# Token affine per head pair, weight sums and attention steps moved: a block-sorted attention followed by a token and channel MLP

## The chip, the cores and the metric

The kernel runs on one core of one Trainium2 chip. Its engines work side by side, each with its own queue that is worked off in order: TensorE (PE: matrix products into PSUM; its weight loads are shown as PEld), VectorE (DVE), ScalarE (ACT), GpSimd (POOL), and SyncE (SP), which here does nothing but issue DMA transfers. The metric is the device time of one execution in microseconds (us), the median over several runs. A profile of one execution gives, instruction by instruction, when each engine worked and what it waited for.

## The reference

Two blocks, one after the other, over batch 4, 8 heads, 768 tokens, 64 channels a head (512 channels in all):

```python
# block-sorted attention: 8 blocks of 96 tokens in each head
P = sort_net                                  # [4, 8, 8, 8]
for _ in range(5):
    P = exp(P - max(P)); P = P / sum(P, -1); P = P / sum(P, -2)
k_sorted = einsum('bhij,bhjcd->bhicd', P, k_blocks)
v_sorted = einsum('bhij,bhjcd->bhicd', P, v_blocks)
x = softmax(q_block @ k_sorted_block.T / 8) @ v_sorted_block      # within a block

# token and channel MLP on x[4, 768, 512]
a1  = alpha1 * x + beta1
tok = einsum('ts,bsd->btd', w_tok, a1)        # over the 768 tokens
u   = x + lam * tok
a2  = alpha2 * u + beta2
ch  = relu(a2 @ w_ch1) @ w_ch2                # 512 -> 2048 -> 512
out = u + lam * ch
```

## The kernel before

**Tiling of the tokens.** [...] The attention works on blocks of 96 tokens: its result `x_of[b]` is a tile [128, 8, 512] whose rows 0 to 95 hold block k in plane k. The token product sums over 768 = 6 x 128 tokens, so planes 0 to 5 have to be full: rows 96 to 127 of plane k are filled with a third (32 rows) of block 6 or 7. `tails(x, lo, hi, eng)` (line 513) does that in three copies, the a-th from rows 32a to 32a+31 of planes 6 and 7 to rows 96 to 127 of planes a and a+3. The token weights are permuted to the same order at the start. `a1_of[b]` is a tile of the same form and holds alpha1 * x + beta1, already multiplied by lam and a constant gain of 64.

**Attention steps.** A batch has four head pairs g = 0 to 3, and each has two halves hf (blocks 0 to 3, 4 to 7). `score(b, g, hf)` (line 419) issues 8 matrix products and one exponential on ACT (tile `et`); `pv(b, g, hf)` (line 479) issues 8 products with the values `Vs`, then on DVE a reciprocal and a multiplication that writes x. Both take their PSUM from a pool `psA` of two buffers. After its x, `pv` puts the affine of its 96x4x128 corner (`first_affine`, line 443: a multiplication and an addition on DVE) into a list `late`. In batch 1 each `pv` empties the list (`flush`); in batches 2 and 3 `flush_one` (line 510) takes one entry at a given place.

**The channel part.** Its hidden layer is computed in two halves hf of 384 tokens: `h_unit` (line 761) is one of 16 hidden units (4 products, then a relu on ACT), with PSUM from a pool `psB` of four buffers, shared with the token products and the output products. The outputs of batch 0 are plain products (`ch_unit`, line 764: three row tiles kk in four parts each). Batches 1 to 3 use a scheme with seven products in place of eight for a pair of row tiles (`ch_pair`, line 829): it needs differences of the second weight matrix, made once on DVE (`block_weights`, line 796: eight differences of 128x1024 into the tiles TWa and TWb), and sums and differences of hidden tiles (`block_sums`, line 812: four DVE operations for each range lo to hi of 8, three pairs n = 0, 1, 2 a batch). In `ch_pair` the accumulator px is used for three products and pz for two; each later product waits until the addition on DVE (`add_out`, line 791) has read the one before. Half 0 has the pair n = 0, half 1 the pairs n = 1 and 2.

**The token layer.** `moe_tok(b, kt)` (line 713): six products over a1, then on DVE u = x + tok / 64, then on ACT a cast of u to f16. `moe_cross(b, hf)` (line 723) issues three DMA transposes of u on SP; `moe_affine(b, hf)` (line 730) makes the input a2T of the hidden units from them, four operations on DVE, or on ACT for half 1 of batches 1 to 3.

**Keys and values of the next batches.** `mix_v` (line 545) and `mix_k` (line 560), three of each a batch, multiply the raw values and keys with the sorting matrices; ACT copies the results out of PSUM (one cast for values, four for keys). `bounce_v` sends the mixed values to memory in two DMAs and `back_v` brings them back as `Vs`; `q_cross` transposes the queries in six DMAs; all of these are issued by SP. `loads` waits on POOL until `Vs` has come back and then loads the raw tensors of the batch after that.

**The order is written out by hand.** Every engine gets its instructions in program order. The main loop goes over b and hf; each (b, hf) runs its 16 hidden units and after unit i what is registered for (b, hf, "h", i); then the output products, and after each product (or part) what is registered for (b, hf, "c", n). `put(b, hf, kind, n, ...)` (line 963) registers. So attention of batch b is spread over the channel part of batch p = b - 1, key and value mixing of b over the output products of (p - 1, 1), and the token layer of b over (p, 1) and (b, 0). The places in question stand in lines 998 to 1041: `put(p, *at_, flush_one)` at 1016, the pairs of scores and values at 1009, the tails at 1017, `block_weights` at 1033, `block_sums` of pair 2 at 1040.

Of the kernel before, what the change touches and what calls it, by code (L numbers as in the profile page):

```python
# [16 lines left out]
def kernel(  # L17
# [24 lines left out]
    BLK = S // NB  # L42
# [400 lines left out]
    def first_affine(b, rows, kts, c):  # L443
        n = kts.stop - kts.start
        w = c.stop - c.start
        dst = a1_of[b][rows, kts, c]
        al, be = (
            t_[rows, c].unsqueeze(1).to_broadcast([rows.stop - rows.start, n, w]) for t_ in (alphaB, betaB)
        )
        dve.tensor_tensor(dst, x_of[b][rows, kts, c], al, ALU.mult)  # L450
        dve.tensor_tensor(dst, dst, be, ALU.add)
# [27 lines left out]
    def pv(b, g, hf):  # L479
        if g == 0 and hf == 0:  # L480
            x_of[b] = moep.tile([128, 8, C], F16, name="x128", tag="x128", bufs=1)
            a1_of[b] = moep.tile([128, 8, C], F16, name="a1", tag="a1", bufs=1)
        ps = psa([128, 2, 512], FT, "x_ps")[:].rearrange("p a (k d) -> p a k d", d=128)
        et = ets[(b, g, hf)][:].rearrange("p a i t -> p (a i t)")
        for ii in range(4):
            for h2 in range(2):
                lo = (4 * h2 + ii) * BLK
                w = min(128, 8 * BLK - lo)
                pe.matmul(
                    ps[0:w, h2, ii, 0:D + 1], et[0:BLK, lo:lo + w],  # L490
                    Vs[0:BLK, (2 * g + h2) * NB + 4 * hf + ii, 0:D + 1], start=True, stop=True,
                )
        rc = att.tile([128, 2, 4], FT, name="rcb", tag="rc", bufs=3)
        dve.reciprocal(rc[0:BLK], ps[0:BLK, :, :, D])
        dve.tensor_tensor(
            x_of[b][0:BLK, 4 * hf:4 * hf + 4, g * 128:(g + 1) * 128].rearrange("p k (a d) -> p k a d", a=2),
            ps[0:BLK, :, :, 0:D].rearrange("p a k d -> p k a d"),
            rc[0:BLK].rearrange("p a k -> p k a").unsqueeze(3).to_broadcast([BLK, 4, 2, D]), ALU.mult,
        )
        if b == 1:  # L500
            flush()
        late.append(lambda: first_affine(b, slice(0, BLK), slice(4 * hf, 4 * hf + 4), slice(g * 128, (g + 1) * 128)))

    late = []

    def flush():
        while late:
            late.pop(0)()
# [1 line left out]
    def flush_one():  # L510
        late.pop(0)()

    def tails(x, lo, hi, eng):
        flush()
        for a in range(3):
            eng(x[96:128, a:a + 4:3, lo:hi], x[32 * a:32 * a + 32, 6:8, lo:hi])

    def q_cross(b, kt):
        if kt == 0:
# [40 lines left out]
    def mix_k(b, n, engs):  # L560
        if n == 0:
            kT_of[b] = att.tile([128, H4, NB, BLK], F16, name="kT", tag="kT", bufs=1)
        ps = psa([128, 8, 128], FT, "kmix_ps")
        raw = raw_of[(b, 0)]
        for tp in range(8):
            pe.matmul(
                ps[:, tp, :], raw[:, 16 * n + 2 * tp:16 * n + 2 * tp + 2, :].rearrange("p t d -> p (t d)"),
                bigP[b][:].rearrange("p a t g i -> p (a t g i)"), start=True, stop=True,
            )
        dst = kT_of[b][:].rearrange("p g i (th tp par) -> p th (g i) tp par", th=2, par=2)  # L570
        for par in range(2):
            for h2 in range(2):
                engs[2 * par + h2](
                    dst[h2 * 64:h2 * 64 + 64, :, :, 8 * n:8 * n + 8, par],
                    ps[par * 64:par * 64 + 64, :, h2 * 64:h2 * 64 + 64].rearrange(
                        "p n (th c) -> p th c n", th=2
                    ),
                )
# [134 lines left out]
    def moe_tok(b, kt, ps):  # L713
        u32 = u_of[b]
        tok_part(b, kt, 0, C, ps)
        if b not in u16_of:
            u16_of[b] = moep.tile([128, NT, C], F16, name="u16", tag="u16", bufs=1)
        dve.scalar_tensor_tensor(
            u32[kt], tok_of[(b, kt)][:], 1.0 / GAIN, x_of[b][:, kt, :], op0=ALU.mult, op1=ALU.add,
        )  # L720
        act.copy(u16_of[b][:, kt, :], u32[kt])
# [8 lines left out]
    def moe_affine(b, hf):  # L730
        for ci in range(CT):
            affine(b, hf, ci, uT_of[(b, hf)][:, ci, :], act if b and hf else dve)
# [230 lines left out]
    def put(b, hf, kind, n, *todo):  # L963
        at.setdefault((b, hf, kind, n), []).extend(todo)
# [19 lines left out]
    for b in range(1, B):  # L984
        p = b - 1
        if b == 1:
            for n in range(3):
                put(0, 0, "h", 11 + n, lambda n=n: mix_v(1, n, act.copy))
                put(0, 0, "c", 3 + 3 * n, lambda n=n: mix_k(1, n, (act.copy,) * 4))
            put(0, 0, "h", 13, lambda: bounce_v(1))  # L990
            put(0, 0, "c", 1, lambda: back_v(1))
            for g in range(H4):
                put(0, 0, "c", (4, 7, 10, 10)[g], lambda g=g: q_turn_late(1, g, (dve.tensor_copy, act.copy)[g % 2]))
            put(0, 0, "c", 11, lambda: loads(2))
            seq = [("s", 0), ("s", 1), ("s", 2), ("p", 0), ("s", 3), ("p", 1), ("p", 2), ("s", 4), ("p", 3), ("s", 5),
                   ("p", 4), ("s", 6), ("p", 5), ("s", 7), ("p", 6), ("p", 7)]
            for at_, (kind, n) in enumerate(seq):
                put(0, 1, "h", at_, (lambda n=n: score(1, n // 2, n % 2, psa)) if kind == "s" else (lambda n=n: pv(1, n // 2, n % 2)))
        else:
            for n in range(3):  # L1000
                put(p - 1, 1, "c", 1 + n, lambda b=b, n=n: mix_v(b, n, act.copy))
                put(p - 1, 1, "c", 5 + (2, 3)[b - 2] * n, lambda b=b, n=n: mix_k(b, n, (act.copy,) * 4))
            put(p - 1, 1, "c", 3, lambda b=b: bounce_v(b))
            put(p - 1, 1, "c", 7, lambda b=b: back_v(b))
            for kt in range(NT):
                put(*((0, 1, "h", 13) if b == 2 else (1, 0, "c", 1)), lambda b=b, kt=kt: q_cross(b, kt))
            if b + 1 < B:
                put(p, 0, "h", 3, lambda b=b: loads(b + 1))
            for (kind, n), at_ in zip(
                pairs, ((0, "h", 1), (0, "h", 4), (0, "h", 6), (0, "h", 8), (0, "h", 10), (0, "h", 12), (0, "h", 14), (0, "c", 3)),  # L1010
            ):
                for i in range(2):
                    f = (lambda b=b, n=n + i: score(b, n // 2, n % 2, psa)) if kind == "s" else (lambda b=b, n=n + i: pv(b, n // 2, n % 2))
                    put(p, *at_, f)
            for at_ in ((0, "h", 7), (0, "h", 9), (0, "h", 11), (0, "h", 13), (0, "c", 1), (0, "c", 5), (1, "h", 0), (1, "h", 1)):
                put(p, *at_, flush_one)
        put(
            p, 1, "h", 15 if b == 1 else 2, lambda b=b: tails(a1_of[b], 0, C, dve.tensor_copy),
            lambda b=b: tails(x_of[b], 0, C, dve.tensor_copy),
        )  # L1020
        put(p, 1, "h", 3, lambda b=b: moe_start(b))
        for kt in range(3):
            put(p, 1, *(("c", 4) if b == 1 else ("h", 5 + 2 * kt)), lambda b=b, kt=kt: moe_tok(b, kt, psb))
        put(p, 1, *(("c", 4) if b == 1 else ("h", 9)), lambda b=b: moe_cross(b, 0))
        put(p, 1, "c", 8 if b == 1 else 6, lambda b=b: moe_affine(b, 0))
        for kt in range(3):
            put(b, 0, "h", 2 * kt, lambda b=b, kt=kt: moe_tok(b, 3 + kt, psb))
        put(b, 0, "h", 4, lambda b=b: moe_cross(b, 1))
        put(b, 0, "c", 0, lambda b=b: moe_affine(b, 1))

    for g, m in enumerate((12, 12, 13, 13)):
        put(0, 0, "h", m, lambda g=g: scale_weights(g))
    for n, at_ in enumerate(((0, 1, "h", 13), (0, 1, "h", 14), (0, 1, "h", 15), (0, 1, "c", 1), (0, 1, "c", 6), (0, 1, "c", 9), (0, 1, "c", 11), (1, 0, "h", 5))):
        put(*at_, lambda n=n: block_weights(n))
    for b in range(1, B):
        for hf in range(2):
            for at_, lo, hi in ((8, 0, 4), (14, 4, 7), (15, 7, 8)):
                at.setdefault((b, hf, "h", at_), []).insert(0, lambda b=b, hf=hf, lo=lo, hi=hi: block_sums(b, hf, lo, hi))
        put(b, 1, "h", 11, lambda b=b: block_sums(b, 2, 0, 4))
        for at_, lo in ((1, 4), (4, 6)):  # L1040
            put(b, 1, "c", at_, lambda b=b, lo=lo: block_sums(b, 2, lo, lo + 2))

    for m in range(3):
        h_part(0, 0, m, [0])
# [58 lines left out]
```

## Time and profile before

| | us |
|---|---|
| median of 3 runs (264.88 to 266.41) | 266.05 |
| the profiled execution | 265.02 |
| its span, first instruction to last | 263.2 |

| engine | busy, us | share of the span |
|---|---|---|
| TensorE (PE) | 248.8 | 95% |
| VectorE (DVE) | 180.0 | 68% |
| ScalarE (ACT) | 154.7 | 59% |
| GpSimd (POOL) | 44.1 | 17% |

The granted clock of TensorE was 1.0 throughout. How to read the lines that follow: all engines' instructions are recorded by one helper, so every line number is L65 (SPq is SyncE's queue, and its rows are DMA issues); an instruction is told by its tiles, "output <- inputs", with partitions x elements and type. On a timeline the first column is the start in us after the span's start, the second the length, and a bracket at the end is idle time ahead of it with what ended it. Neighbouring DVE instructions overlap by some 0.07 us at their ends, so that a price is better taken from start to start.

In time the kernel runs so: batch 0's attention and everything that is loaded once until about 35 us; the channel part of batch 0 until 103 (half 1 from 70, with batch 1's attention in it); batch 1 from 104 to 161 (half 0 with batch 2's attention to 132, half 1 after it); batch 2 from 161 to 216; batch 3 to the end.

### The profile page before, as it was taken

The numbers are of one execution on the slowest core, as the hardware profiler recorded it, in microseconds if no ns is written. First come the engines' busy times: TensorE is split into PE (matmuls) and PEld (weight loads), VectorE is DVE, ScalarE is ACT, GpSimd is POOL, SyncE is SP. The second block draws the span as 40 slices with busy tenths as digits, with TensorE's granted clock in tenths as the row PEclk, the third lists the DMA queues.
The fourth block names the chain that finished last, engine by engine and source line by source line (L and its number), as shares of the span: only waits on it lengthen the run. The fifth ranks groups of instructions, "written<-read, shape, count | busy, mean of one in ns | idle before, by whom it ended". The sixth has DMA issues, their size and how long they took to land.

```text
span 263.2 us, 5966 instructions
## 1 busy us (share of the span) xinstructions
PE 248.8 (95%) x2371; PEld 159.9 (61%) x2371; DVE 180.0 (68%) x473; ACT 154.7 (59%) x282; POOL 44.1 (17%) x67
## 2 busy tenths in 40 slices
PE   7998899999999998998999999998999999999994
PEld 3466565545556444555855797556756875686783
DVE  6796979486359973469996774289977862361863
ACT  3577766657987549777446578788156004747400
POOL 8759304400181000083000000000000000000000
PEclk9999999999999999999999999999999999999999
DMA  6999999998999956989972169500122123111022
GB/s 103 214 203 190 206 205 214 200 135 184 193 167 170 130 137 153 152 139 176 159 124 69 22 157 161 125 20 2 41 59 42 42 82 80 23 38 42 2 80 80
DMA packets 67535, 31.07 MB, mean 118 GB/s; under 512 B 56674, under 2 KB 63218, under 8 KB 67508
## 3 DMA queue, kind: packets, MB, share of 16 engines
q0 software_dynamic: 26352, 15.34, 44.8%
q1 hardware_dynamic: 41060, 15.33, 33.0%
q8 instruction: 18, 0.29, 0.4%
q14 instruction: 9, 0.07, 0.1%
q10 hardware_dynamic: 96, 0.03, 0.1%
HBM read 32.79 MB, written 8.65 MB: 157 GB/s over the span
## 4 chain that ended last, share of the span: by engine, by line
PE 53%; DVE 17%; ACT 4%; issue 2%; DMA 1%; SPq 0%; DVEq 0%; ACTq 0%
PE h_ps L65 21%; PE tok_ps L65 8%; PE px L65 6%; PE pz L65 5%; PE py L65 5%; DVE x L65 4%; DVE sums L65 4%; PE ch_ps L65 3%; DVE a L65 3%; DVE ost L65 2%; ACT et L65 2%; PE sc_ps L65 1%; DVE hTa L65 1%; ACT kT L65 1%; PE kmix_ps L65 1%
## 5 line engine op out<-in xcount | busy, mean ns | idle before, releaser
L65 PE MATMUL h_ps<-a2T,W1p 128*128 128x384 bf16 x512 | 94.5, 327 | 0.9 <-DVE a2T L65 0.9
L65 PEld LDWEIGHTS <-W1p 128*128 128x128 bf16 x512 | 47.7, 98 | 32.9 <-issue 1.8
L65 ACT ACTIVATE hTa<-h_ps 128x384 f16<-128x384 f32 x64 | 31.2, 493 | 32.3 <-PE h_ps L65 31.7
L65 ACT ACTIVATE hTb<-h_ps 128x384 f16<-128x384 f32 x64 | 31.1, 489 | 8.1 <-PE h_ps L65 8.1
L65 PE MATMUL tok_ps<-a,w_tokT 128*128 128x512 f16 x126 | 30.7, 379 | 0.6 <-DVE ost L65 0.6
L65 DVE SCALAR_TENSOR_TENSOR u<-tok_ps,x 128x512 f32<-128x512 f32 x21 | 14.4, 691 | 22.5 <-PE tok_ps L65 22.5
L65 ACT CAST kT<-kmix_ps 64x512 f16<-64x512 f32 x36 | 25.7, 713 | 6.3 <-PE kmix_ps L65 5.8
L65 ACT CAST u<-u 128x512 f16<-128x512 f32 x21 | 12.9, 617 | 24.5 <-DVE u L65 24.5
L65 ACT ACTIVATE et<-sc_ps 96x768 f16<-96x768 f32 (+1 forms) x32 | 25.0, 807 | 2.0 <-PE sc_ps L65 1.8
L65 PEld LDWEIGHTS <-sums 128*128 128x128 f16 x216 | 21.1, 98 | 5.7 <-issue 2.7
L65 PEld LDWEIGHTS <-hTb 128*128 128x128 f16 x200 | 18.7, 98 | 6.6 <-issue 0.8
L65 PEld LDWEIGHTS <-hTa 128*128 128x128 f16 x192 | 18.5, 98 | 6.6
L65 PEld LDWEIGHTS <-w_tokT 128*128 128x128 f16 x126 | 12.3, 98 | 14.1 <-issue 1.5
L65 DVE TENSOR_TENSOR sums<-hTa,hTb 128x512 f16<-128x512 f16 (+3 forms) x27 | 8.9, 329 | 12.1 <-ACT hTb L65 11.8
L65 DVE TENSOR_TENSOR x<-x_ps,rcb 96x512 f16<-96x512 f32 x24 | 16.5, 686 | 0.8
L65 POOL DMA_DIRECT2D qn<-in_q_dram x18 | 16.0, 906 | 5.3 <-DMA raw<-in_v_dram 4.8
L65 PEld LDWEIGHTS <-et 96*128 96x128 f16 (+4 forms) x288 | 12.1, 100 | 6.2 <-issue 2.3
L65 PE MATMUL x_ps<-Vs,et 96*128 96x65 f16 (+4 forms) x288 | 13.4, 195 | 2.5 <-ACT et L65 1.1
L65 DVE TENSOR_TENSOR a<-a,betaB 96x512 f16<-96x512 f16 (+1 forms) x28 | 12.3, 441 | 1.0
L65 DVE SCALAR_TENSOR_TENSOR ost<-px,u 128x256 f32<-128x256 f32 x27 | 11.2, 417 | 2.2 <-PE px L65 2.2
L65 PE MATMUL warm_ps<-wz 128*128 128x512 f16 x36 | 11.1, 441 | 1.2 <-DVE wz L65 1.2
L65 PE MATMUL ch_ps<-W2p,hTb 128*128 128x512 f16 x48 | 12.0, 379 | 0.2
(140 smaller groups left out, 354.3 us busy)
## 6 DMA issues: line engine op xcount, KB each, us to landing
out_dram<-ost SPq DMA_DIRECT2D x23, 192.0 KB, 2.5
raw<-in_v_dram POOLq DMA_DIRECT2D x6, 384.0 KB, 7.2
raw<-in_k_dram POOLq DMA_DIRECT2D x6, 384.0 KB, 9.8
qn<-in_q_dram POOLq DMA_DIRECT2D x18, 128.0 KB, 10.7
vscr<-mixed SPq DMA_DIRECT2D x6, 384.0 KB
Vs<-vscr SPq DMA_DIRECT2D x3, 768.0 KB
W1p<-in_moe_w_ch_dram POOLq DMA_DIRECT2D x4, 512.0 KB, 11.8
W2p<-in_moe_w_ch_dram POOLq DMA_DIRECT2D x4, 512.0 KB, 17.3
```

The lines of the kernel that those rows point to most:

```text
L65: ins = getattr(self.eng, name)(*args, **kwargs)
```

## The change

The affine is no longer made per half pair but once per head pair: the second `pv` of a pair registers three copies of x that fill the tails of that pair's 128 channels, and then one affine over all 128 rows and six planes. The six copies over all channels (three of a1, three of x) go. In batches 2 and 3 the entries are taken at other places. The scores and values of batches 2 and 3 stand at other units and steps, two of the steps now in the output products, and the last values in half 1. The eight weight differences go behind batch 1's token products, in two groups of four. The key mixes of batches 2 and 3 stand one or more steps earlier, the first three token products of batches 2 and 3 and their transposes two units later, the affine of half 1 two steps later, and the sums of pair 2 are cut otherwise.

```diff
@@ pv
         if b == 1:
             flush()
-        late.append(lambda: first_affine(b, slice(0, BLK), slice(4 * hf, 4 * hf + 4), slice(g * 128, (g + 1) * 128)))
+        if hf == 1:
+            c = slice(g * 128, (g + 1) * 128)
+            late.append(lambda: tails(x_of[b], c))
+            late.append(lambda: first_affine(b, slice(0, 128), slice(0, NT), c))
@@ tails
-    def tails(x, lo, hi, eng):
-        flush()
+    def tails(x, c):
         for a in range(3):
-            eng(x[96:128, a:a + 4:3, lo:hi], x[32 * a:32 * a + 32, 6:8, lo:hi])
+            dve.tensor_copy(x[96:128, a:a + 4:3, c], x[32 * a:32 * a + 32, 6:8, c])
@@ the places
-                put(p - 1, 1, "c", 5 + (2, 3)[b - 2] * n, lambda b=b, n=n: mix_k(b, n, (act.copy,) * 4))
+                put(p - 1, 1, "c", ((3, 6, 8), (4, 7, 10))[b - 2][n], lambda b=b, n=n: mix_k(b, n, (act.copy,) * 4))
...
-                pairs, ((0, "h", 1), (0, "h", 4), (0, "h", 6), (0, "h", 8), (0, "h", 10), (0, "h", 12), (0, "h", 14), (0, "c", 3)),
+                pairs, ((0, "h", 0), (0, "h", 3), (0, "h", 5), (0, "h", 8), (0, "h", 11), (0, "c", 0), (0, "c", 2), (1, "h", 1)),
...
-            for at_ in ((0, "h", 7), (0, "h", 9), (0, "h", 11), (0, "h", 13), (0, "c", 1), (0, "c", 5), (1, "h", 0), (1, "h", 1)):
+            for at_ in ((0, "h", 6), (0, "h", 7), (0, "h", 12), (0, "h", 13), (0, "c", 4), (0, "c", 5), (1, "h", 2), (1, "h", 3)):
                 put(p, *at_, flush_one)
-        put(
-            p, 1, "h", 15 if b == 1 else 2, lambda b=b: tails(a1_of[b], 0, C, dve.tensor_copy),
-            lambda b=b: tails(x_of[b], 0, C, dve.tensor_copy),
-        )
+        if b == 1:
+            put(p, 1, "h", 15, flush)
         put(p, 1, "h", 3, lambda b=b: moe_start(b))
         for kt in range(3):
-            put(p, 1, *(("c", 4) if b == 1 else ("h", 5 + 2 * kt)), lambda b=b, kt=kt: moe_tok(b, kt, psb))
-        put(p, 1, *(("c", 4) if b == 1 else ("h", 9)), lambda b=b: moe_cross(b, 0))
+            put(p, 1, *(("c", 4) if b == 1 else ("h", 7 + 2 * kt)), lambda b=b, kt=kt: moe_tok(b, kt, psb))
+        put(p, 1, *(("c", 4) if b == 1 else ("h", 11)), lambda b=b: moe_cross(b, 0))
...
-        put(b, 0, "c", 0, lambda b=b: moe_affine(b, 1))
+        put(b, 0, "c", 2, lambda b=b: moe_affine(b, 1))
...
-    for n, at_ in enumerate(((0, 1, "h", 13), (0, 1, "h", 14), (0, 1, "h", 15), (0, 1, "c", 1), (0, 1, "c", 6), (0, 1, "c", 9), (0, 1, "c", 11), (1, 0, "h", 5))):
+    for n, at_ in enumerate(((0, 1, "c", 7),) * 4 + ((0, 1, "c", 9),) * 4):
         put(*at_, lambda n=n: block_weights(n))
...
-        for at_, lo in ((1, 4), (4, 6)):
-            put(b, 1, "c", at_, lambda b=b, lo=lo: block_sums(b, 2, lo, lo + 2))
+        for at_, lo, hi in ((0, 4, 7), (5, 7, 8)):
+            put(b, 1, "c", at_, lambda b=b, lo=lo, hi=hi: block_sums(b, 2, lo, hi))
```

In the list of pairs, s0, s2, s4, s6 are the scores of head pairs 0 to 3 (both halves), p0, p2, p4, p6 their values, in the order s0, s2, p0, s4, p2, s6, p4, p6.

## The prediction

> **What bounds the kernel now.** I read the page's head first, then TensorE's (PE's) waits from 69 us on, where the diff begins to act, and then the timelines of VectorE (DVE) and SyncE's queue (SPq) at each wait.
>
> ```profile
> span 263.2 us, 5966 instructions
> PE 248.8 (95%) x2371; PEld 159.9 (61%) x2371; DVE 180.0 (68%) x473; ACT 154.7 (59%) x282; POOL 44.1 (17%) x67
> ```
>
> PE sets the time. The change adds and removes no matmul, so it can only win what PE waits, or lose by new waits. The waits of PE after 69 us (waited for: total, times, longest):
>
> ```profile
> PE sc_ps L65 <- DVE x L65: 1.3, 4, 0.5
> PE x_ps L65 <- ACT et L65: 1.1, 4, 0.3
> PE h_ps L65 <- DVE a2T L65: 0.9, 1, 0.9
> PE px L65 <- DVE ost L65: 0.8, 2, 0.4
> PE pz L65 <- DVE ost L65: 0.7, 2, 0.3
> PE tok_ps L65 <- DVE ost L65: 0.6, 1, 0.6
> ```
>
> They sum to 5.4 us. On PE's timeline they lie in four places: 0.63 before the third token product of batch 1 (94.61) and 0.91 before its first hidden unit (104.36); 0.28, 0.28, 0.17, 0.49 and 0.39 in batch 1, half 0; 0.28, 0.28, 0.17, 0.49 and 0.38 in batch 2, half 0; 0.34 and 0.33 in the output products of half 1 of batches 2 and 3. The first hidden unit also takes 1.19 us instead of 0.65, as its four inputs come one by one: 0.54 more. So about 5.9 us are in reach, 2.2%.
>
> The rows that price the DVE work (timeline: start, length, instruction):
>
> ```profile
> 76.85 0.41 DVE L65 TENSOR_TENSOR a<-x,alphaB 96x512 f16<-96x512 f16 x1
> 77.29 0.42 DVE L65 TENSOR_TENSOR a<-a,betaB 96x512 f16<-96x512 f16 x1
> 77.64 0.20 DVE L65 RECIPROCAL rcb<-x_ps 96x8 f32<-96x8 f32 x1
> ...
> 89.96 1.32 DVE L65 COPY a<-a 32x1024 f16<-32x1024 f16 x3
> 91.31 1.32 DVE L65 COPY x<-x 32x1024 f16<-32x1024 f16 x3
> 92.66 1.29 DVE L65 TENSOR_TENSOR TWa<-W2p,TWa 128x1024 f16<-128x1024 f16 x2
> 93.87 0.69 DVE L65 SCALAR_TENSOR_TENSOR ost<-ch_ps,u 128x512 f32<-128x512 f32 x1
> ```
>
> **The affine and the tails.** Now an affine of one half pair takes 0.44 + 0.35 = 0.79 from start to start, eight of them 6.3 us a batch, and six copies 89.96 to 92.66 = 2.7: 9.0 us. After, a pair takes two operations over 128x768, which batch 0 shows (starts 39.28, 39.86, 40.34: 0.58 + 0.48 = 1.06), and three copies of 32x256. No row has such a copy. Below, the shortest DVE row is 0.16 (a 16x16 cast); above, the same copy with four times the elements, 0.42. Between the SBUF copies 128x128 (0.224) and 32x1024 (0.421) a line gives 0.25 at 256 elements; I take that. A pair is then 0.75 + 1.06 = 1.81, a batch 7.2 us: 1.7 less. The copies themselves save nothing (12 x 0.25 = 3.0 against 2.7): half the elements, twice the instructions. DVE is 68% busy, so this counts only where PE waits on it, and inside the hidden part each pair costs 0.24 more than its two affines do now.
>
> [...]
>
> **Place 1, the token layer of batch 1.** DVE runs unbroken from 82.96 to 94.5; the add that frees the PSUM buffer for the third token product ends there (93.87 above). Ahead of it go away four weight differences (0.61 each, 2.45) and 1.7 of affine and tails: it could start at 89.7, so it starts at the product's end, 89.9. The 0.63 falls. The key mix of batch 2 now stands ahead of the token products, 0.45 of PE work that only changes place: they run 91.7 to 95.6.
>
> **Place 2, the first hidden unit of batch 1.** Its input goes u, f16 cast (ACT), three DMA transposes (SPq), DVE affine. The queue now:
>
> ```profile
> 84.34 8.57 SPq L65 DMA_TRANSPOSE qT<-qn  x6
> 94.58 0.79 SPq L65 DMA_DIRECT2D out_dram<-ost  x2
> 95.46 1.10 SPq L65 DMA_DIRECT2D vscr<-mixed  x2
> 96.65 5.92 SPq L65 DMA_TRANSPOSE uT<-u  x3
> ```
>
> SPq is in order: the bounce of the mixed values waits behind a store that waits for that same add, and the first transpose takes 3.3 us to issue instead of 1.2, until some 4.5 us after the bounce. After, the store goes at 92.95, when the six query transposes are through. The bounce has a new wait: on ACT, four key casts (2.9 us, 90.4 to 93.3) now stand ahead of the last value cast (1.0), so it goes at 94.35, 1.1 earlier than now; behind it on SPq wait the three transposes. The u casts follow on ACT (last one 96.3 to 96.9, now 96.83 to 97.45), no later than now. The transposes move by 1.1 to 1.25, the last lands at 102.6 instead of 103.8, the hidden unit starts at 103.1. PE would be there at 102.6, so 0.5 of the wait is left. Places 1 and 2 together: **-1.25**. Bounds: 0 (bounce no earlier) to -2.3 (PE's own 1.75 and the 0.54).
>
> **Place 3, the weight sums.** Eight differences leave the attention half for two groups of four. The first (2.5 us) falls into DVE's idle stretch before the affine of place 2 (4.10 us idle there now): nothing; without that cover it would be 2.5 us on place 2. The second stands behind that affine, two more than now (1.2 us). Queued behind it are the last add of batch 0 and the first u of the new half. The add ends at 107.1; the third hidden unit needs its buffer and would start at 106.95: **+0.2**, bounds 0 and 1.2.
>
> **Place 4, half 0 of batches 1 and 2.** The values of steps p0 come a score pair and more after their exponentials, s6 and its wait on DVE move to the output products: 1.61 and 1.60 of waits fall. What is late next: DVE. By the rows of now PE takes 0.65 for a hidden unit (1.19 for the first), 1.30 for a token product, 0.45 for a score pair and some 0.1 at each change of kind: from 103.1, with the 0.2 of place 3, p0 runs at 113.0 to 113.4 and the last hidden unit ends at 121.2. From p0 (x rows 0.84 each) to the end of the hidden part it has two pairs of x (3.4), two pairs of copies and affine (3.6) and the block sums (1.7, 1.35, 0.8): 10.9 us from 113.4, thus until 124.2, 3.0 us after PE's last hidden unit (now 2.7). Then three adds and the x rows of p4, moved to step 2, 1.7 us, stand ahead of the add that frees px for its third product: done at 127.5 (three adds 1.2, x rows 1.7, its own 0.42), while PE gets there at 126.8 (five products of 0.87, s6 0.45, p4 0.54, changes 0.25). New wait **0.75** a batch, so -0.86 and -0.85. Bounds of the wait: 0.2 (the six copies ahead of it at 0.16) to 1.8 (at 0.42). The token product now starts two hidden units later, 134.75 against an input ready at 134.2: no wait, 0.55 slack. Scores at slot 0 need the last key cast; the key mixes are a slot or more earlier, done by 103.8 on ACT, before PE asks at 104.65. The values' return (issue to landing 8.6 us now: 103.84 to the gate at 112.45) lands near 111, p0 comes at 113. The ACT affine of half 1 moves from step 0 to 2 behind two exponentials; its input landed at 126.1, PE needs it at 129: nothing.
>
> **Place 5, half 1.** Tokens at units 7, 9, 11 push a block sum behind the last of them, and three quarters of the rest now go in the first step (1.35 instead of 1.1, and ahead of two adds): +0.2 in batch 2, +0.1 in batch 3; in batch 1 the mixes' PE work covers it.
>
> **Sum:** -1.25 + 0.2 - 0.86 - 0.85 + 0.3 = -2.46: span 260.7. The profiled execution took 265.0 (1.8 around its span), 1.0 under the median 266.05; I carry the difference to the median: **263.6 us**.
>
> **Rivals.** (A) DVE becomes the bound of half 0 (slower). Place: end of the hidden part of batches 1 and 2. Each us by which DVE ends the block sums later goes on PE twice through px. From 1.23 us more than worked out, the gain is gone; at 2.0 more the sum is +1.5, 267.6. For: the adds have no room now either (px already waits 0.39). Against: the copies' far bound alone gives 1.0. (B) No gain to measure: the bounce is no earlier, and the px wait replaces the five waits (1.6): +0.2 + 0 + 0 + 0.3, 266.5; with only the copies at 0.42 it is 265.7. For: SPq, not the add, holds the transposes. (C) Better: copies at their low bound, PE takes all of place 2: -2.3 + 0.2 - 1.41 - 1.40 + 0.3 = -4.6, 261.4. For: nothing but the queues holds PE there. Against: the bounce's new wait. A part that does not do what it seems to is in the sum: the copies.
>
> **How the numbers follow.** Forecast 0.55, C 0.15, B 0.17, A 0.13. Three runs before span 1.5 us, and 0.5% (1.3 us) is about what a measurement tells from no change: faster 0.70, same 0.17, slower 0.13. The range goes from C's time, less half a us for its own spread, to between B and A: 260.9 to 267.0.
>
> **What would show it.** Third token product without a wait; hidden unit near 103; copies 32x256 near 0.25; a wait of PE on px of 0.5 to 1.0 in the output products of half 0, twice, and none on sc_ps or x_ps. Wrong if px waits exceed 2 us, or if the bounce goes after 95.5.

## The result, and the profile after

The changed kernel takes **262.62 us** (median of 4 runs, 262.48 to 263.29), against 265.92 (264.88 to 266.41) for the kernel before beside it: ratio **0.9886, interval 0.9852 to 0.992**. The prediction was 263.6, range 260.9 to 267.0, faster by over 0.5%. Beside the experiments below the kernel before took 265.07 to 265.28 (medians of 18, 7 and 13 runs), so the 265.92 of its four runs here is high: against those the fall is some 2.5 us and not 3.3, though they did not run beside the changed kernel.

The head of the page after:

```profile
span 260.8 us, 5951 instructions
PE 248.4 (95%) x2371; PEld 159.8 (61%) x2371; DVE 175.0 (67%) x467; ACT 154.6 (59%) x282; POOL 44.3 (17%) x67
```

PE's work is the same; DVE has 5.0 us less of it. PE's waits from 69 us on (waited for: total, times, longest), where there were six rows with 5.4 us:

```profile
PE px L65 <- DVE ost L65: 2.1, 3, 1.0
PE pz L65 <- DVE ost L65: 1.1, 2, 0.7
PE h_ps L65 <- DVE a2T L65: 0.6, 1, 0.6
```

3.8 are left: sc_ps, x_ps and tok_ps are gone, px has grown from 0.8 to 2.1. The three px waits on PE's timeline after (start, length, instruction, idle before it):

```profile
125.79 1.03 PE L65 MATMUL px<-TWa,sums 128*128 128x256 f16 x8 [0.19 <-DVE ost L65]
...
128.65 1.03 PE L65 MATMUL px<-TWb,hTa 128*128 128x256 f16 x8 [0.95 <-DVE ost L65]
...
183.59 1.03 PE L65 MATMUL px<-TWb,hTa 128*128 128x256 f16 x8 [0.95 <-DVE ost L65]
```

SyncE's queue after, around the hidden unit of batch 1:

```profile
93.17 0.99 SPq L65 DMA_DIRECT2D out_dram<-ost  x2
95.39 1.10 SPq L65 DMA_DIRECT2D vscr<-mixed  x2
96.58 5.74 SPq L65 DMA_TRANSPOSE uT<-u  x3
```

The store no longer waits for the add of the token layer, and the bounce of the mixed values goes right after ACT's last value cast. ACT's timeline after shows the new wait that the prediction had put there, the key casts ahead of that cast:

```profile
91.46 2.87 ACT L65 CAST kT<-kmix_ps 64x512 f16<-64x512 f32 x4 [0.30 <-PE kmix_ps L65]
94.35 1.01 ACT L65 CAST mixed<-mix_ps 128x1024 f16<-128x1024 f32 x1
```

**Where the time went.** PE's timeline can be cut at the first hidden unit and at the first output product of each half; nothing is lost between the cuts. I worked out this table from those starts (us; half 0 carries the next batch's attention):

| stretch | before | after | difference | predicted |
|---|---|---|---|---|
| batch 0 half 1, hidden part (attention of batch 1) | 15.82 | 16.21 | +0.39 | 0 |
| batch 0 half 1, output part and wait for the hidden unit (places 1, 2) | 18.75 | 17.61 | -1.14 | -1.25 |
| batch 1 half 0, hidden | 20.23 | 17.58 | | |
| batch 1 half 0, output | 7.43 | 8.72 | -0.84 for both | -0.66 |
| batch 1 half 1 | 29.24 | 29.66 | -0.10 | 0 |
| batch 2 half 0, hidden | 19.85 | 16.97 | | |
| batch 2 half 0, output | 7.42 | 8.31 | -1.47 for both | -0.85 |
| batch 2 half 1 | 27.31 | 28.01 | +0.18 | +0.2 |
| batch 3 | 47.40 | 47.45 | +0.05 | +0.1 |
| sum | | | **-2.93** | -2.46 |

In batches 1 and 2 the value pair that moves from half 0 to half 1 takes 0.52 of PE's work with it (x_ps at 131.69, the next unit at 132.20); it is taken out of the differences. The span fell by only 2.4 because this execution was 0.48 later when it came to 36 us, where no edit has acted: its warm-up matmuls took 466 ns instead of 441 in the mean. So 260.8 against the predicted 260.7 is in part luck. The hidden unit of batch 1 starts at 104.10 and not near 103, for the same 0.48, the 0.39 of the first row and the 0.11 that the second row falls short. The predicted time lies 1.0 us over the measured one because the prediction added 1.0 for a median above the profiled execution: after the change the two are 262.62 and 262.59.

### The profile page after: what moved, and what is told of

Same layout as the page of the kernel before. It is cut to its first block, busy times and chain, and to the rows that moved or that the text cites. A ratio compares the mean times of both kernels' runs of the same rounds, so it can differ in the third digit from the quotient of the medians.

```text
span 260.8 us, 5951 instructions
## 1 busy us (share of the span) xinstructions
PE 248.4 (95%) x2371; PEld 159.8 (61%) x2371; DVE 175.0 (67%) x467; ACT 154.6 (59%) x282; POOL 44.3 (17%) x67
## 4 chain that ended last, share of the span: by engine, by line
PE 54%; DVE 19%; issue 2%; SPq 1%; DMA 1%; ACT 0%; DVEq 0%; ACTq 0%
PE h_ps L65 20%; PE tok_ps L65 9%; PE px L65 7%; DVE x L65 6%; PE py L65 5%; PE ch_ps L65 5%; DVE sums L65 4%; PE pz L65 4%; DVE a L65 2%; DVE ost L65 2%; DVE hTa L65 1%; PE kmix_ps L65 1%; PE x_ps L65 1%; PE sc_ps L65 1%; SPq L65 1%
## 5 line engine op out<-in xcount | busy, mean ns | idle before, releaser
L65 DVE TENSOR_TENSOR sums<-hTa,hTb 128x512 f16<-128x512 f16 (+2 forms) x27 | 8.9, 328 | 10.0 <-ACT hTb L65 10.0
L65 PE MATMUL warm_ps<-wz 128*128 128x512 f16 x36 | 11.9, 466 | 1.2 <-DVE wz L65 1.2
L65 ACT CAST mixed<-mix_ps 128x1024 f16<-128x1024 f32 x9 | 9.1, 1013 | 4.9 <-PE mix_ps L65 4.8
```

Source lines behind the costliest of these rows:

```text
L65: ins = getattr(self.eng, name)(*args, **kwargs)
```

## The experiments

Each kernel ran beside the kernel before on one chip; "from 70 us" means from the first hidden unit of batch 0's half 1 to the end, as in the table (193.45 before, 190.51 after), which leaves the start out. These differences come from one profiled execution each. In the texts put on record before each run, M is the theory held and R or W its rival. First the three parts, each alone on the kernel before.

**The weight differences alone.**

```diff
-    for n, at_ in enumerate(((0, 1, "h", 13), (0, 1, "h", 14), (0, 1, "h", 15), (0, 1, "c", 1), (0, 1, "c", 6), (0, 1, "c", 9), (0, 1, "c", 11), (1, 0, "h", 5))):
+    for n, at_ in enumerate(((0, 1, "c", 7),) * 4 + ((0, 1, "c", 9),) * 4):
```

> The kernel before with one part of the change: the eight weight differences behind the token products of batch 1. Theory M (the gain of that place comes from the add that frees the token product's buffer, and from the store and the bounce queued behind it on SyncE's queue): the add comes 2.45 us earlier, at about 92.0, the third token product does not wait (-0.63), the bounce goes at about 93.8 since no key casts stand ahead of its value cast, the first hidden unit of batch 1 finds its input there (-0.91 and -0.54), and the second group of four costs 0.2 to 0.5 at the third unit: -1.6 us in all (-1.0 to -2.1), nothing after 110 us. Rival W (the freed DVE time has no path to TensorE without the affine per pair, since the tails of 2.7 us still stand ahead of that add): within 0.3 us of before.

Measured 264.28 against 265.07: 0.9963 (0.9949 to 0.9976); from 70 us 192.60, 0.85 less. PE's timeline:

```profile
103.16 1.19 PE L65 MATMUL h_ps<-a2T,W1p 128*128 128x384 bf16 x4 [0.32 <-DVE a2T L65]
...
110.44 1.46 PE L65 MATMUL tok_ps<-a,w_tokT 128*128 128x512 f16 x6 [0.35 <-ACT hTa L65]
```

Places 1 and 2 gain 1.39 (the stretch takes 17.36 instead of 18.75): the whole of what the change wins there, and without the affine per pair. The second row is place 3: the second group of four stands on DVE ahead of the next u, so ACT's cast of that u starts 4.45 after the first hidden unit instead of 3.25, and the token product waits for a relu behind it on ACT; 0.51 more in that stretch. The mechanism is right; its size on the whole is under the expectation.

**The affine and the tails per pair alone.**

```diff
-        late.append(lambda: first_affine(b, slice(0, BLK), slice(4 * hf, 4 * hf + 4), slice(g * 128, (g + 1) * 128)))
+        if hf == 1:
+            c = slice(g * 128, (g + 1) * 128)
+            late.append(lambda: tails(x_of[b], c))
+            late.append(lambda: first_affine(b, slice(0, 128), slice(0, NT), c))
```

> The kernel before with the affine and the tails per head pair alone, at the places of before. Theory M: the add ahead of the third token product comes 1.7 us earlier, which is enough for it and for the store, so place 1 and 2 gain up to 2.1 as in the run with the weights alone; batch 1's attention loses 0.4 (two waits of TensorE on a buffer while a whole pair is made ready); half 0 of batches 1 and 2 keeps its waits, up to 0.3 longer each. In all -1.0 us (-1.7 to -0.3). Rival R (the gain of the whole change is DVE work saved, 5 us of busy time): -2.4 us, all of it.

Measured 265.75: 1.0019 (1.0006 to 1.0032); from 70 us 194.00, 0.55 **more**. Both expectations fall. Places 1 and 2 gain 1.26 (17.49), nearly as much as with the weight differences: either of the two is enough. But the attention of batch 1 loses 0.53, the hidden part of batch 1's half 0 loses 1.03 and that of batch 2 loses 0.32. DVE's timeline in batch 1, PE's there, and PE's before:

```profile
116.30 1.57 DVE L65 COPY x<-x 32x256 f16<-32x256 f16 x3
```

```profile
121.53 0.34 PE L65 MATMUL sc_ps<-qT,kT 64*128 64x96 f16 x8 [1.38 <-DVE x L65]
122.37 0.35 PE L65 MATMUL sc_ps<-qT,kT 64*128 64x96 f16 x8 [0.49 <-DVE x L65]
```

```profile
121.00 0.34 PE L65 MATMUL sc_ps<-qT,kT 64*128 64x96 f16 x8 [0.17 <-DVE x L65]
```

Three copies take 1.57 instead of some 0.7 (a run on that stands further down), stand ahead of the x rows, and the wait of the scores for the PSUM buffer, 0.17 before, becomes 1.38. In batch 2, where no copy takes longer than 0.3, that wait is 0.49: so part of the loss in batch 1 is the long copies.

**The moved steps alone**, with affine, tails and weight differences as before.

```diff
-                pairs, ((0, "h", 1), (0, "h", 4), (0, "h", 6), (0, "h", 8), (0, "h", 10), (0, "h", 12), (0, "h", 14), (0, "c", 3)),
+                pairs, ((0, "h", 0), (0, "h", 3), (0, "h", 5), (0, "h", 8), (0, "h", 11), (0, "c", 0), (0, "c", 2), (1, "h", 1)),
...
```

> The kernel before with the places alone (attention steps, key mixes, tokens, affine of half 1, sums of pair 2), the affine per half pair and the weight differences where they were. Theory M: places 1 and 2 gain nothing (bounce near 95.5, first unit near 104.4); half 0 loses its waits on sc_ps and x_ps and keeps a px wait of about 0.5 a batch (a pair is 0.24 us cheaper on DVE than in the whole change), about -1.2 in batch 1 and -1.7 in batch 2; the token products of half 1 wait 0 to 0.5 for tails that are now later: -2.4 us in all (-1.8 to -3.0). Rival R (DVE work saved is the gain): within 0.7 us of before, since DVE does the same work.

Measured 262.39: 0.9902 (0.9879 to 0.9924); from 70 us 190.68, **2.77 less**. The two largest of PE's waits that are left; none is on sc_ps or x_ps:

```profile
PE px L65 <- DVE ost L65: 1.4, 2, 0.9
PE h_ps L65 <- DVE a2T L65: 1.3, 1, 1.3
```

Places 1 and 2 gain next to nothing here (18.64, the bounce at 95.58); half 0 gains it, 1.53 in batch 1 and 1.99 in batch 2 (the 0.52 of the moved value pair taken out), and the halves 1 after them give 0.26 and 0.54 back. M holds: most of the whole gain without a single DVE operation saved. The run moves all the steps together; what each of the moves is worth by itself is not shown.

The parts add up in total, -0.85 + 0.55 - 2.77 = -3.07 against -2.93 for the change, but not place by place: at places 1 and 2 they make -2.76 against -1.14, since two of them take the same wait away, and in half 0 of batch 1 (without the moved pair's 0.52) +0.13 against -0.84. That the sums are so close is a coincidence.

**Is DVE really the chain in half 0?** The changed kernel, with the tail copies of batches 2 and 3 made twice:

```diff
-        for a in range(3):
+        for a in list(range(3)) * (2 if x is not x_of[1] else 1):
```

> The whole change with every tail copy of batches 2 and 3 done twice (24 copies of 32x256 more, 0.23 us each). Theory M (DVE's lag at the end of the hidden part goes on TensorE one for one through px): two pairs of copies stand ahead, 1.4 us, so the px wait goes from 0.95 to about 2.3 in half 0 of batches 1 and 2, and the token products of half 1 wait up to 0.8 a batch, their slack being some 0.3: 3 to 4.4 us over the changed kernel. Rival (DVE is idle a third of the time and takes it up): within 0.7 us of the changed kernel.

Measured 269.09: 1.0136 (1.0109 to 1.0164). PE's waits:

```profile
PE pz L65 <- DVE sums L65: 2.8, 4, 1.2
PE tok_ps L65 <- DVE a L65: 1.7, 2, 1.0
```

More than M's 3.0 to 4.4. Not all of it is the copies: in this execution the granted clock was 0.72 from 128 to 134 us (windows view: length, busy time of PE, PEld, DVE, ACT and POOL, granted clock, DMA share, GB/s).

```profile
128.00:134.00 6.00, 5.81 (x49) 4.55 (x49) 5.21 (x18) 1.82 (x4) 0.00 (x0) 0.72 2.34 161
```

That lies in batch 1's half 0, whose loss can't be taken as it stands: 0.28 of 6 us would be 1.7, but the slower products (the px row there takes 1.50 instead of 1.03) also filled the wait on px (the add ended at 131.69, the product started at 131.84), so an estimate of what the clock cost is 0.6: that 0.15 and the 0.46 by which the product then took longer than 0.87. Batch 2 ran at full clock: its output part and token layer lose 2.7 (1.58 + 1.14) for 12 copies that cost DVE 3.0 (0.25 each from start to start). So a microsecond on DVE there costs PE 0.9, once: some in the output part, where block sums come late, and the rest at the token layer, whose affine is last in the line. The px wait itself stays at 0.95, so M's path is not the one taken. It is not paid twice through px, as rival A had it.

**What is left of place 2.** The changed kernel with the last value mix ahead of the last key mix, in batches 2 and 3:

```diff
             for n in range(3):
                 put(p - 1, 1, "c", 1 + n, lambda b=b, n=n: mix_v(b, n, act.copy))
+            for n in range(3):
                 put(p - 1, 1, "c", ((3, 6, 8), (4, 7, 10))[b - 2][n], lambda b=b, n=n: mix_k(b, n, (act.copy,) * 4))
```

> The changed kernel, with the last value mix of batch 2 (and of batch 3) ahead of its last key mix, so that ACT casts the values before the four key rows. M (what is left of the first hidden unit's wait stands on the bounce of the mixed values, and the bounce on ACT): the bounce goes near 94.3 instead of 95.4, the first hidden unit of batch 1 starts 0.6 to 1.0 earlier (near 103.3) without its 0.56 of wait: the time 0.6 to 1.1 us under the changed kernel, span 259.7 to 260.2. R (the transposes behind the bounce are held by the queue itself, some 4.5 us after the stores of batch 0, not by the bounce): the bounce goes earlier but the last transpose and the hidden unit stay within 0.2 of 104.1, span 260.6 to 261.0.

Measured 261.32: 0.9848 (0.9825 to 0.987). SyncE's queue:

```profile
83.88 8.77 SPq L65 DMA_TRANSPOSE qT<-qn  x6
92.75 1.00 SPq L65 DMA_DIRECT2D out_dram<-ost  x2
93.84 1.10 SPq L65 DMA_DIRECT2D vscr<-mixed  x2
95.26 5.57 SPq L65 DMA_TRANSPOSE uT<-u  x3
```

The bounce goes at 93.84, right behind the store, and the list of PE's waits has none on a2T any more: places 1 and 2 take 16.88 instead of 17.61, 0.73 less. M holds, near its lower end. What stands ahead of the bounce now is the line of six query transposes; the queue itself has become the holder.

**The px wait.** The changed kernel with the fifth value product one output step later:

```diff
-                pairs, ((0, "h", 0), (0, "h", 3), (0, "h", 5), (0, "h", 8), (0, "h", 11), (0, "c", 0), (0, "c", 2), (1, "h", 1)),
+                pairs, ((0, "h", 0), (0, "h", 3), (0, "h", 5), (0, "h", 8), (0, "h", 11), (0, "c", 0), (0, "c", 3), (1, "h", 1)),
```

> The changed kernel, with the fifth value product of the attention of batches 2 and 3 one output step later (3 instead of 2), so that its x rows on DVE (0.84 each) stand behind the add that frees px and not ahead of it. M (the px waits of 0.95 are those x rows): both px waits fall to 0.2 or less; -0.8 a stage, span 259.0 to 259.5, ratio to the kernel before 0.980 to 0.983. R (DVE is late as a whole at the end of the hidden part, by about 3 us, and the next thing that needs it waits instead): the waits come back on pz or on the first hidden unit of half 1, 0.5 or more each, and the span stays above 260.2.

Measured 262.10: 0.9878 (0.9856 to 0.9899), span 260.4; from 70 us 190.23, 0.28 less. The wait of 0.95 goes, but PE waits longer on px two products earlier (0.19 in the changed kernel, and in batch 2 0.36 where it had none):

```profile
125.91 1.03 PE L65 MATMUL px<-TWa,sums 128*128 128x256 f16 x8 [0.70 <-DVE ost L65]
...
128.17 1.04 PE L65 MATMUL px<-TWb,hTa 128*128 128x256 f16 x8
```

Output parts 0.39 and 0.60 shorter, half 1's hidden parts 0.31 longer each: DVE's last affine (135.31 to 135.87) now ends just ahead of the token product (135.93), which PE reached 0.3 earlier. R holds in its sum, not in its places: the lateness moves on to the earlier px product and to the tokens, and 0.28 is won. The x rows in front of the add were mostly the place where it came out.

**The affine per pair taken out of the changed kernel.** The reverse of the second experiment's diff on the changed kernel.

> The changed kernel with the affine and the tail rows as they were before the change (an affine for each half pair, six copies of 1024 at the end); weight differences and attention steps stay moved. M (the affine per pair wins nothing: it costs 0.4 in the attention of batch 1 and 0.5 of px in each half 0, and gives back some 0.36 in each half 1): the time 0.2 to 0.8 us under the changed kernel, span 260.0 to 260.6. R (the 1.7 us of DVE work that the affine per pair saves a batch is part of the gain, as the prediction's places 1 and 2 have it): 0.5 to 1.2 us slower than the changed kernel, span 261.3 to 262.0, with a wait before the third token product of batch 1 again.

Measured 261.83: 0.9861 (0.9833 to 0.9889); from 70 us 189.45, 1.06 **less** than the changed kernel. PE's waits:

```profile
PE pz L65 <- DVE ost L65: 1.1, 2, 0.7
PE px L65 <- DVE ost L65: 0.9, 2, 0.4
PE h_ps L65 <- DVE a2T L65: 0.6, 1, 0.6
```

M holds in the profile: batch 1's attention -0.39, the output parts of half 0 -0.94 and -0.53, the token layers +0.35 each. Of the 0.94 some 0.4 is the one long copy of batch 1 in the changed kernel's execution (0.63 instead of 0.22). The third token product has no wait without it either. The ratio to the changed kernel can't be told from one by the intervals; the signs of this and of the second experiment agree.

**Batch 1's attention.** The changed kernel, with one entry of the late list let out at each value product, not all:

```diff
-        if b == 1:
-            flush()
+        if b == 1 and late:
+            flush_one()
```

> The changed kernel, in which a value product of batch 1 lets out one entry of the list of late DVE work (the copies, or the affine) instead of all of it. M (batch 1's attention lost 0.4 because a pair's copies and affine, 1.8 us, stand in one piece before the next x rows, and the PSUM buffer that these free comes late to PE): the attention half of batch 1 goes back from 16.21 to 15.8, span 260.3 to 260.5. R (it is the sum of DVE's work there, not where it stands): 16.1 to 16.3 and the span within 0.15 of the changed kernel's 260.8.

Measured 262.17: 0.9876 (0.9857 to 0.9896). The attention half falls from 16.21 to 15.60, under the 15.82 of before: M is right on the cause. But the profiled execution gave 0.40 back in the output part of batch 1's half 0 (9.12 against 8.72): ahead of it two of three copies took 0.64 and 0.62 (one of 0.63 in the changed kernel); from 70 us 190.34.

**Why some copies take three times as long.** The changed kernel, each tail copy written as the maximum of the rows with themselves, which reads two sources:

```diff
-            dve.tensor_copy(x[96:128, a:a + 4:3, c], x[32 * a:32 * a + 32, 6:8, c])
+            s = x[32 * a:32 * a + 32, 6:8, c]
+            dve.tensor_tensor(x[96:128, a:a + 4:3, c], s, s, ALU.max)
```

> The changed kernel, with each tail copy of 32x256 written as the maximum of the rows with themselves, which reads two sources. M (a one-source f16 copy of DVE shares something with POOL, whose DMA issues at 71 to 81 and 112 to 121 us hold it up; an operation with two sources doesn't): no tail row longer than 0.3 us, at 116 us too, where the copy took 0.63; time within 0.4 of the changed kernel, span 260.4 to 261.0. R (the rows are slow there for any operation, from the transfers into SBUF at that time): rows of 0.4 to 0.7 at 112 to 121 us remain, as with the copies.

Measured 263.40: 0.9926 (0.9903 to 0.995). DVE's timeline, the changed kernel and then this one, and POOL's of this one:

```profile
115.84 1.10 DVE L65 COPY x<-x 32x256 f16<-32x256 f16 x3
...
121.42 0.69 DVE L65 COPY x<-x 32x256 f16<-32x256 f16 x3
```

```profile
116.13 0.88 DVE L65 TENSOR_TENSOR x<-x 32x256 f16<-32x256 f16 x3
...
121.48 0.88 DVE L65 TENSOR_TENSOR x<-x 32x256 f16<-32x256 f16 x3
```

```profile
114.96 4.42 POOL L65 DMA_DIRECT2D qn<-in_q_dram  x5
```

All 36 two-source rows take 0.28, beside POOL's issues as elsewhere. M holds for the rows: the lengthening belongs to the one-source copy, and R, slow rows for any operation, falls. That it is POOL's issuing which lengthens them rests on the times alone: no run moves the issues. M's time fails: the span is 261.5, not 260.4 to 261.0, and from 70 us it is 191.50, 0.99 more than the changed kernel's, most of it in the attention of batch 1 and the output part of batch 2's half 0 (0.38 each). That fits a row that costs 0.06 more on the chain; no run shows that this is all.

**Earlier value products.** The changed kernel with the first two value products and the fourth score pair of batches 2 and 3 a hidden unit earlier:

```diff
-                pairs, ((0, "h", 0), (0, "h", 3), (0, "h", 5), (0, "h", 8), (0, "h", 11), (0, "c", 0), (0, "c", 2), (1, "h", 1)),
+                pairs, ((0, "h", 0), (0, "h", 3), (0, "h", 4), (0, "h", 7), (0, "h", 10), (0, "c", 0), (0, "c", 2), (1, "h", 1)),
...
-            for at_ in ((0, "h", 6), (0, "h", 7), (0, "h", 12), (0, "h", 13), (0, "c", 4), (0, "c", 5), (1, "h", 2), (1, "h", 3)):
+            for at_ in ((0, "h", 5), (0, "h", 6), (0, "h", 11), (0, "h", 12), (0, "c", 4), (0, "c", 5), (1, "h", 2), (1, "h", 3)):
```

> The changed kernel, with the first two value products and the fourth score pair of batches 2 and 3 one hidden unit (0.65 us) earlier, and the copies and affine of the first two pairs with them. M (from the first value product to the token layer of half 1 DVE is the chain, and PE waits on px for what DVE is late): the px waits of 0.19 + 0.95 and 0.95 fall by about 0.65 each, span 259.2 to 259.7, 0.8 to 1.4 us under the changed kernel. R (the px wait comes from the place of the fifth product's x rows alone, right ahead of the add; earlier work on DVE doesn't move it): px waits of 0.8 or more stay, span 260.5 to 261.0.

Measured 261.78: 0.9871 (0.9856 to 0.9886); from 70 us 189.93, 0.58 less. PE's timeline in batch 1:

```profile
113.53 0.42 PE L65 MATMUL x_ps<-Vs,et 96*128 96x65 f16 x8 [0.28 <-ACT et L65]
...
128.20 1.03 PE L65 MATMUL px<-TWb,hTa 128*128 128x256 f16 x8 [0.59 <-DVE ost L65]
```

Between the two: the px wait of 0.95 falls by 0.36 in batch 1, where the 0.19 goes too, and by 0.30 in batch 2, not by 0.65. In batch 1 the add that makes u from the third token product stands on DVE ahead of the first x rows: they begin 9.65 after the first hidden unit instead of 9.95 (113.61 and 114.05), only 0.30 earlier. And a wait for an exponential that the change had removed is back, 0.28.

**Combined.** The changed kernel without the affine per pair and with the value mix first; and the same with the earlier value products.

> The changed kernel without the affine per pair, and with the last value mix of batches 2 and 3 ahead of the last key mix: the two edits that each gained alone. M (they act at different places: the mixing of batch 2, and the attention steps): the gains add, 0.8 and 0.7 to 1.3: time 260.3 to 261.1, ratio to the kernel before 0.979 to 0.983, span 1.8 less than the changed kernel's from the first hidden unit of batch 0 on (223.1). R (the earlier start of the half after finds DVE no earlier, so the waits on px and the tokens take one of the gains back): 261.3 or more.

> The one before, with the first two value products and the fourth score pair of batches 2 and 3 one hidden unit earlier too. M (DVE is the chain from the first value product on): px waits of 0.4 to 0.5 and the 0.35 of the token products of half 1 go, 0.6 to 1.4 us less than the kernel without this step. R (the values' return holds the first product: it lands 0.7 to 0.8 before PE asks for it, hardly more than the 0.65 of the move, or PE's buffers for the scores come late): within 0.3 of the one before, with a wait on Vs, sc_ps or x_ps in its place.

Measured 261.46, 0.9851 (0.9815 to 0.9887), and 261.53, 0.9875 (0.9827 to 0.9924). In the first the gains don't add, and not for R's reason. SyncE's queue:

```profile
85.35 8.83 SPq L65 DMA_TRANSPOSE qT<-qn  x6
94.27 1.00 SPq L65 DMA_DIRECT2D out_dram<-ost  x2
95.36 1.10 SPq L65 DMA_DIRECT2D vscr<-mixed  x2
```

The six query transposes end 7.6 us into the output part; with the value mix alone they ended at 6.8, and the bounce is right behind them. So in this execution the second holder decides there. This kernel's four spans are 258.7, 259.1, 260.2 and 260.5; that the short ones are those with early transposes is not shown. The profiled execution of the second has the shortest way of all, 188.78 from 70 us, with a bounce at 94.13, but its runs reach from 260.79 to 263.64. None of these is shown to beat the changed kernel; the lowest ratio with a narrow interval is that of the value mix first alone.

## Why the prediction was right, point by point

**Places 1 and 2** (-1.25; measured -1.14). The token product without a wait, the bounce behind four key casts, and about half a microsecond left before the hidden unit (0.56) are as worked out; the bounce moved by 0.95 within the stretch instead of 1.1. But the reason given was too wide: the four weight differences alone bring 1.39, the affine and the tails per pair alone 1.26, and together they bring no more. The kernel with differences and steps moved and the affine as before takes 17.66 there, the changed kernel 17.61.

**Place 3** (+0.2): the size is right, the path is not. Two kernels differ in the place of the weight differences alone, the one with the steps alone and the changed one with the affine as before: the hidden part of batch 1 takes 17.35 and 17.58, 0.23 more. But the third hidden unit, where the prediction put it, does not wait (106.96 in the changed kernel, with the unit before it, 1.31 for the two). ACT's timeline after, and PE's:

```profile
108.55 0.62 ACT L65 CAST u<-u 128x512 f16<-128x512 f32 x1 [2.67 <-DVE u L65]
109.07 1.50 ACT L65 ACTIVATE et<-sc_ps 96x768 f16<-96x768 f32 x2
```

```profile
110.31 0.66 PE L65 MATMUL sc_ps<-qT,kT 64*128 64x96 f16 x16
111.00 0.81 PE L65 MATMUL h_ps<-a2T,W1p 128*128 128x384 bf16 x4
```

The u behind the differences comes late, so ACT casts it 4.45 after the first hidden unit instead of 3.25 with the steps alone; the exponentials and relus behind that cast are late, and the next scores take 0.69 to the next hidden unit where 0.44 is free. That this costs the 0.2 of the prediction is luck.

**Place 4** (-0.86 and -0.85; measured with place 3 -0.84, and -1.47). The step "1.61 and 1.60 of waits fall" was mis-sized. PE's timeline before, in batch 2:

```profile
169.50 1.48 PE L65 MATMUL h_ps<-a2T,W1p 128*128 128x384 bf16 x8
171.26 0.41 PE L65 MATMUL x_ps<-Vs,et 96*128 96x65 f16 x8 [0.28 <-ACT et L65]
171.96 0.42 PE L65 MATMUL x_ps<-Vs,et 96*128 96x65 f16 x8 [0.28 <-ACT et L65]
172.21 1.47 PE L65 MATMUL h_ps<-a2T,W1p 128*128 128x384 bf16 x8
```

Two hidden units occupy 1.30 when nothing waits, though their row says 1.48: the next matmul starts some 0.17 before the modelled end. The first x_ps comes 1.76 after them, so it was held 0.46, and its bracket says 0.28; the second starts 0.70 after the first where 0.25 is free, held 0.45. Each bracket on PE leaves out about 0.17 here. Five waits of 1.60 cost 2.45, and the new px wait of 0.95 costs 1.12 (183.59 is 1.99 after the product that took 0.87). That gives -1.33 for batch 2 (-1.47 measured); batch 1, with 0.19 and 0.95 of px and the 0.2 of place 3, is at -0.78 (-0.84 measured). The 0.14 left in batch 2 stays open. The px wait itself was 0.95 and not 0.75, inside its bounds: DVE ended the block sums 3.3 us after PE's last hidden unit in batch 2 and 3.7 in batch 1, where one copy took 0.63, and not 3.0.

**Batch 1's attention** (no cost; measured +0.39). The prediction saw that "inside the hidden part each pair costs 0.24 more" and put it at nothing in its sum. What counts there is that copies and affine come in one piece ahead of the next x rows: 78.35 to 80.14 on DVE, while PE's next value product waits for the buffer. Letting them out one by one takes it away.

**Place 5** (+0.3; measured +0.18, +0.05 and in batch 1 -0.10, +0.13 together) is right for batch 2, and so are the **copies** (0.25; their rows are 0.22, apart from those beside POOL's issues).

**The rivals.** A's mechanism is there, a chain on DVE through half 0, but at one time its lag and not twice; it didn't decide, as the copies were at the low side. B falls: the bounce was earlier, and px took back less than the five waits gave. C's -4.6 would have needed PE to take all of place 2 and next to no wait on px.

So the two misses, batch 1's attention (+0.4) and the waits counted short (-0.2 and -0.6), partly cancel: the nearness of -2.46 to -2.93 is in part luck. Of the three parts one that was counted as a gain, the affine per pair, is a loss: 0.55 alone on the kernel before, where the runs agree (1.0006 to 1.0032), and 1.06 within the change, there by one profile each.

## What to carry to other kernels

Each wait in PE's list was short by about 0.17 here, since the next matmul starts that much before the modelled end of the row ahead: read a wait from start to start, and count the waits as well as their sum. Less work on an engine that isn't the bound gained here only where the bound waited for it, and then once, whichever piece of work went (at places 1 and 2 1.39 or 1.26 for one piece alone, 1.14 in the whole change); put in one piece ahead of an operation that frees a PSUM buffer, the lesser work cost 0.55 in all. Parts that add up in total need not add up place by place. Ask for every chain what is second in line: here the holders that went (the add, the key casts, the x rows) each had another close behind.

## What the runs showed of the hardware

**DVE copies beside POOL's DMA issues.** The f16 copy of 32x256 with one source takes 0.22 us; while POOL issues its loads (71 to 81 and 112 to 121 us) single ones take 0.42 to 0.69, others there the usual 0.22: 0.63 in the changed kernel, 0.69 and 0.63 in the kernel with the affine per pair alone, 0.64 and 0.62 with the entries let out one by one. With the copies made twice, batch 1's attention, which that edit leaves alone, had rows of 0.42 and 0.63 (78.46, 79.14) and was 0.6 longer. Away from POOL's issues all copies of the changed kernel take 0.22, and the rows with two sources took 0.28 beside them and away from them. What the copy and POOL's issues share no row shows.

**The clock.** In one execution (copies made twice) the granted clock was 0.72 from 128 to 134 us and 1.0 in the stretches before and after; a profile's loss has to be looked at for that before it is put down to an edit. By the estimate above it cost 0.6 and not the 1.7 that is missing of those 6 us, since part of it filled a wait on px.
